# Banded attention of an attention and feed-forward chain: shared-key value products by column halves, the group's result finished over three steps, and copies of P on two engines

## Chip, core and metric

The kernel runs on one core of one Trainium2 chip. The metric is the device time of one execution in microseconds, and the median of 3 runs of the kernel before is 637.89 us (637.67 to 638.56).

## What is computed

```python
def _attn_ref(q, k, v, n_sink, window):          # q, k, v: 2 batches, 8 heads, 768 positions, 64 wide
    scores = np.matmul(q, k.transpose(0, 1, 3, 2)) / np.sqrt(D)
    keep = (pos_k < n_sink) | ((rel >= 0) & (rel < window))      # n_sink 4, window 128
    scores = np.where(keep, scores, -1e9)
    a = np.exp(scores - np.max(scores, axis=-1, keepdims=True))
    return np.matmul(a / (np.sum(a, axis=-1, keepdims=True) + 1e-09), v)

def reference(...):
    x = attention, heads side by side             # 1536 tokens x 512
    h = x @ w_in;  x = softplus(h) @ w_out        # 512 -> 2048 -> 512
    h = x @ w2_in; return (h * clip(h + 3, 0, 6) / 6) @ w2_out
```

## The kernel before

**Attention.** The 1536 tokens are 12 groups `g` of 128 queries (6 blocks `i` in each of 2 batches). A group is worked in two quads of 4 heads, so the loop of `banded_attention` has 24 steps `n` (`g, quad = divmod(n, 2)`) and 3 more in which the pipeline runs empty. For a block other than the first a query sees 208 columns: 128 keys that both halves of the queries share (the upper half of the block before and the lower half of its own), and 80 that belong to one half of the queries (64 of its own and 16 sink keys). Scores are fp32 products (`scores`, L480 and L487) into two PSUM tiles of a pool of three. `exps` takes one head at a time: VectorE adds the mask and takes the row's extreme (L500), ScalarE takes the exponential and its sum (L504). One step later TensorE turns P (`transposes`, L518): four 128x128 pieces into PSUM tile `pt` 0 and four of 80 columns into `pt` 1. VectorE copies the first tile (L526, 128x512), ScalarE the second (L528, 80x512). One step later still come the value products: `apply_x` (L538) for the shared keys, with all 128 queries as the stationary operand, and `apply_y` (L551) for the others, in halves of 64 queries, each half writing its own 64 partitions of the result `o`.

**Finishing a group.** After both quads a group's result is normalised (`normalise`, VectorE, L565), turned (`turn_x`, TensorE, L573, into a third use of the `pt` pool) and split in two parts, `store_hi` (ScalarE, L576) and `store_lo` (VectorE, L580). All four stand in one even step `n`, for group `n // 2 - 2`. `inverse` (L559, L560) prepares the divisors.

**Weights.** In some steps (the table `HALVES`) `w.half()` rebuilds one half block of fp32 weights for the feed-forward part from 64-bit words: three VectorE instructions (L97, L100, L103), one on ScalarE (L107) and one on GpSimd (L108). The raw words come by 512 KB transfers on SyncE's queue (L79, L84), four blocks ahead; the first four are issued in step 1, behind the transfers of queries, keys and values. The 32 half blocks of the first weight pair that attention does not rebuild are rebuilt in the first 16 steps of the feed-forward part (`Ffn.filler`).

**Feed-forward.** Every product of 128x128 by 128x512 is written as three of reduced precision. For each of 16 slices `c`, `products` (L145) makes `h`, `activate` (L167 to L177) the activation, and `stage_b` (L202) adds it to four results two slices later. `h` lives in the same pool of three PSUM tiles as the scores, so `h` of slice `c` waits until VectorE's L175 of slice `c - 3` has read its tile. In steps 24 and 25 of the attention loop `products` of slices 0 and 1 are issued already.

**Order.** A wrapper (`in_order`) keeps each engine's instructions of attention and of the first four feed-forward steps in the order in which the program writes them. Behind that a scheduler orders them.

Of the kernel before, what the change touches and what calls it, by code (L numbers as in the profile page):

```python
# [8 lines left out]
F32 = mybir.dt.float32  # L9
# [4 lines left out]
AF = mybir.ActivationFunctionType  # L14
# [4 lines left out]
P = 128  # L19
NEG = 1.0e9  # L20
MAXSINK = 16
HQ = P // 2
SLOTW = P + MAXSINK
YW = HQ + MAXSINK
PW = P + YW
TB = 2
HALVES = (5, 7, 9, 11, 13, 15, 17, 19, 20, 21, 22, 23)
WARM = 22
FIXED = 4

# [338 lines left out]
def banded_attention(ctx, tc, qT_d, kT_d, v, ident, NSv, Wv, xT, psa, isq, w, ffn, flags):  # L369


    nc = tc.nc
    B, H, D, S = qT_d.shape
    NB = S // P
    NG = B * NB
    NP = H // 2
    NQ = 2 * NG

    one = ctx.enter_context(tc.tile_pool(name="a1", bufs=1))
    two = ctx.enter_context(tc.tile_pool(name="a2", bufs=2))  # L380
# [4 lines left out]
    st = {}  # L385
# [48 lines left out]
    r0, r1 = slice(0, HQ), slice(HQ, P)  # L434
# [23 lines left out]
    def scores(n):  # L458
        g, quad = divmod(n, 2)
        i = g % NB  # L460
        s = st[g]
        if quad == 0:
            s["sum"] = two.tile([P, H], F32, tag="sum", name=f"sum_{g}")
            s["mx"] = two.tile([P, H], F32, tag="mx", name=f"mx_{g}")
        s["P", quad] = two.tile([P, 4, PW], F32, tag="P", name=f"P_{n}")
        s["s", quad] = [psa.tile([P, 2, 256], F32, tag="s", name=f"s_{n}_{t}") for t in range(2)]
        for pp in range(2):
            p = quad * 2 + pp
            if i == 0:
                parts = [None]  # L470
            else:
                parts = [(r0, HQ + MAXSINK, P, 0), (r1, HQ + MAXSINK, PW, 0), (r0, 0, YW, P)]
            for part in parts:
                for t in range(2):
                    rows = slice(t * D, (t + 1) * D)
                    ps = s["s", quad][t]
                    if i == 0:
                        for j in range(2):
                            c0 = j * (HQ + MAXSINK)
                            nc.tensor.matmul(  # L480
                                ps[:, pp, j * HQ : (j + 1) * HQ], s["q"][rows, p, :],
                                keys[rows, p, 0, c0 : c0 + HQ], start=True, stop=True,
                            )
                    else:
                        r, lo, n_, at = part
                        lo += (i - 1) * SLOTW
                        nc.tensor.matmul(  # L487
                            ps[r, pp, at : at + n_], s["q"][rows, p, r],
                            keys[rows, p].rearrange("p i c -> p (i c)")[:, lo : lo + n_], start=True, stop=True,
                        )  # L490

    def exps(n, hh):
        g, quad = divmod(n, 2)
        i = g % NB
        s = st[g]
        w_ = P if i == 0 else PW
        mask = m_zero if i == 0 else m_one if i == 1 else m_gen
        h = quad * 4 + hh
        xs = thr.tile([P, PW], F32, tag="xs", bufs=4, name=f"xs_{n}_{hh}")[:, 0:w_]
        nc.vector.tensor_tensor_reduce(  # L500
            out=xs, in0=s["s", quad][hh % 2][:, hh // 2, 0:w_], in1=mask, scale=-isq, scalar=3.0e38,
            op0=ALU.add, op1=ALU.min, accum_out=s["mx"][:, h : h + 1],
        )
        nc.scalar.activation(  # L504
            s["P", quad][:, hh, 0:w_], xs, AF.Exp, scale=-1.0, bias=s["mx"][:, h : h + 1],
            accum_out=s["sum"][:, h : h + 1],
        )

    def transposes(n):

        g, quad = divmod(n, 2)
        i = g % NB
        s = st[g]
        pt = s["P", quad]
        for m, c0, rows in ((0, 0, P), (1, P, YW)) if i else ((0, 0, P),):
            s["ps", m] = pst.tile([P, 512], F32, tag="pt", name=f"pt_{n}_{m}")
            for hh in range(4):
                nc.tensor.transpose(s["ps", m][0:rows, hh * P : (hh + 1) * P], pt[:, hh, c0 : c0 + rows], ident)  # L518

    def copies(n):  # L520
        g, quad = divmod(n, 2)
        s = st[g]
        for m, rows in ((0, P), (1, YW)) if g % NB else ((0, P),):
            t = two.tile([rows, 512], F32, tag=f"PT{m}", name=f"PT_{n}_{m}")
            if m == 0:
                nc.vector.tensor_copy(t, s["ps", m])  # L526
            else:
                nc.scalar.activation(t, s["ps", m][0:rows], AF.Copy)  # L528
            s["T", quad, m] = t

    def apply_x(n):
        g, quad = divmod(n, 2)
        s = st[g]
        if "o" not in s:
            s["o"] = pso.tile([P, H, D], F32, tag="o", name=f"o_{g}")
        for hh in range(4):
            h = quad * 4 + hh
            nc.tensor.matmul(  # L538
                s["o"][:, h, :], s["T", quad, 0][:, hh * P : (hh + 1) * P], s["vx"][:, h, :],
                start=(hh == 0 or g % NB == 0), stop=(g % NB == 0),  # L540
            )

    def apply_y(n):
        g, quad = divmod(n, 2)
        s = st[g]
        if g % NB == 0:
            return
        for hh in range(4):
            h = quad * 4 + hh
            for j, r in enumerate((r0, r1)):  # L550
                nc.tensor.matmul(  # L551
                    s["o"][r, h, :], s["T", quad, 1][:, hh * P + j * HQ : hh * P + (j + 1) * HQ],
                    s["vy"][:, j, h, :], start=False, stop=(hh == 3),
                )

    def inverse(g):
        s = st[g]
        s["rs"] = two.tile([P, H], F32, tag="rs", name=f"rs_{g}")
        nc.vector.tensor_scalar(out=s["rs"], in0=s["sum"], scalar1=1.0e-9, scalar2=None, op0=ALU.add)  # L559
        nc.vector.reciprocal(s["rs"], s["rs"])  # L560

    def normalise(g):
        s = st[g]
        s["x"] = two.tile([P, H, D], F32, tag="x", name=f"x_{g}")
        nc.vector.tensor_tensor(  # L565
            out=s["x"], in0=s["o"], in1=s["rs"].rearrange("p (h o) -> p h o", o=1).to_broadcast([P, H, D]), op=ALU.mult
        )

    def turn_x(g):
        s = st[g]  # L570
        s["xtr"] = pst.tile([P, NP, P], F32, tag="pt", name=f"xtr_{g}")
        for p in range(NP):
            nc.tensor.transpose(s["xtr"][:, p, :], s["x"][:, 2 * p : 2 * p + 2, :].rearrange("p h d -> p (h d)"), ident)  # L573

    def store_hi(g):
        nc.scalar.activation(xT[:, 0, :, g * P : (g + 1) * P], st[g]["xtr"], AF.Copy)  # L576

    def store_lo(g):
        cols = slice(g * P, (g + 1) * P)
        nc.vector.tensor_tensor(  # L580
            out=xT[:, 1, :, cols], in0=st[g]["xtr"], in1=xT[:, 0, :, cols].bitcast(F32), op=ALU.subtract
        )

    def keep_busy(n):

        for _ in range(n):
            nc.tensor.matmul(spare, z[:, 0:P], z, start=True, stop=True)  # L587
# [23 lines left out]
    for n in range(NQ + 3):  # L611
        g, quad = divmod(n, 2)
        new, old, older = n < NQ, 0 <= n - 1 < NQ, 0 <= n - 2 < NQ
        done = n // 2 - 2 if n % 2 == 0 and n >= 4 else None
        if new:
            scores(n)
        elif n - NQ < 2:
            ffn.products("w1", 0, n - NQ)
        if done is not None:
            normalise(done)  # L620
        if n == 0:
            keep_busy(6)
        if new:
            exps(n, 0)
            exps(n, 1)
        if old:
            transposes(n - 1)
            copies(n - 1)
        if new:
            exps(n, 2)  # L630
            exps(n, 3)
        if done is not None:
            turn_x(done)
        if older:
            apply_x(n - 2)
        if done is not None:
            store_hi(done)
        if older:
            apply_y(n - 2)
        if n % 2 == 0 and n >= 2 and n // 2 - 1 < NG:  # L640
            inverse(n // 2 - 1)
        if done is not None:
            store_lo(done)
        if quad == 1 and new:
            if g % NB == 0:
                spread_sinks()
            if g + 2 < NG:
                fetch_v(g + 2)
            if g + 3 < NG:
                fetch(g + 3)  # L650
            if g == 0:
                w.fetch()
        if n == 0:
            masks(1)
        if n == 2:
            flags()
        if n == NQ:
            ffn.activate("w1", "softplus", 0, 0, lambda: None)
        if n in HALVES:
            w.half()  # L660


def dense_attention(ctx, tc, qT_d, kT_d, v, ident, NSv, Wv, xT, isq):
# [112 lines left out]
```

## Time and profile before

| | |
|---|---|
| median of 3 runs | 637.89 us |
| profiled execution | 638.31 us, of which the span from first to last instruction is 636.5 us |
| busy: TensorE, its weight loads | 619.1 us (97%), 513.0 us (81%) |
| busy: VectorE, ScalarE, GpSimd | 329.5 us (52%), 324.9 us (51%), 206.5 us (32%) |
| first feed-forward product starts | 99.42 us |

The profile is of one execution. A busy share over the whole span mixes attention (to about 110 us), in which four engines share the work, with the feed-forward part, in which TensorE is busy nearly all the time. Durations of TensorE's instructions overlap, since they are pipelined: what one costs is the distance from start to start, which the chain of waits shows. The same holds for VectorE and ScalarE to a smaller degree.

### The profile page before, as it was taken

Reading aid. Unit: us, or ns where it says so; the run is one execution under the profiler, and the core shown is the slowest. Engines: PE = TensorE matmul, PEld = TensorE weight load, DVE = VectorE, ACT = ScalarE, POOL = GpSimd, SP = SyncE. Lnnn points to the kernel's source line nnn. Section 1 sums busy time; section 2 is a strip of 40 time slices with the busy share of each in tenths; the row PEclk is TensorE's granted clock in tenths of the full one; section 3 lists DMA queues with packets and bytes.
Section 4 is the critical chain, followed back from the end, with each engine's and each line's share of the span. In section 5 each row is a group of like instructions: output and inputs, shape, how many; then the busy total and the mean of one; then the engine's idle time right before and its main releaser. Section 6 shows DMA issues by size and latency. Waiting matters only on the chain.

```text
span 636.5 us, 9690 instructions
## 1 busy us (share of the span) xinstructions
PE 619.1 (97%) x3612; PEld 513.0 (81%) x3612; DVE 329.5 (52%) x693; ACT 324.9 (51%) x691; POOL 206.5 (32%) x170
## 2 busy tenths in 40 slices
PE   8999889999999999999999999999999999999996
PEld 4888777878888888888888888888888888888884
DVE  5888897899624222235799996222332222322221
ACT  3776766788867655558687853222222222222221
POOL 0011122699854444445889853000000000000000
PEclk9999999999999999999999999999999999999998
DMA  7996776800000000015656530000010000100001
GB/s 192 266 255 175 212 240 231 299 2 1 1 0 2 0 1 0 1 38 161 197 181 198 186 100 1 1 0 1 13 54 2 0 1 0 67 0 1 1 0 71
DMA packets 46599, 50.12 MB, mean 79 GB/s; under 512 B 15248, under 2 KB 37776, under 8 KB 46544
## 3 DMA queue, kind: packets, MB, share of 16 engines
q1 hardware_dynamic: 45312, 49.16, 25.1%
q8 instruction: 30, 0.49, 0.4%
q10 hardware_dynamic: 1232, 0.26, 0.2%
q14 instruction: 25, 0.20, 0.1%
HBM read 46.27 MB, written 3.15 MB: 78 GB/s over the span
## 4 chain that ended last, share of the span: by engine, by line
PE 90%; DVE 5%; issue 2%; ACT 2%; DMA 1%; SPq 0%; DVEq 0%; ACTq 0%
PE y_w L202 40%; PE h_w L145 39%; PE o L538 3%; PE s L487 2%; PE pt L518 2%; PE o L551 2%; DVE x L565 1%; PE spare L587 1%; PE xtr L573 1%; DVE xs L500 1%; DMA raw_w<-in_moe_w_in_dram 1%; PE s L480 1%; DVE t_w L100 0%; DVE PT L526 0%; DVE t_w L103 0%
## 5 line engine op out<-in xcount | busy, mean ns | idle before, releaser
L145 PE MATMUL h_w<-xT,w_w 128*128 128x512 f32 x1152 | 280.8, 389 | 0.8 <-DVE e_w L175 0.8
L145 PEld LDWEIGHTS h_w<-xT,w_w 128*128 128x128 f32 x1152 | 216.0, 188 | 46.1 <-DVE e_w L175 1.3
L202 PE MATMUL y_w<-g_w,w_w 128*128 128x512 f32 x576 | 141.6, 389 | 0.0
L202 PE MATMUL y_w<-w_w,g_w 128*128 128x512 f32 x576 | 138.9, 389 | 0.0
L202 PEld LDWEIGHTS y_w<-w_w,g_w 128*128 128x128 f32 x576 | 108.0, 188 | 23.1 <-ACT g_w L182 0.4
L202 PEld LDWEIGHTS y_w<-g_w,w_w 128*128 128x128 f32 x576 | 108.2, 188 | 22.4
L108 POOL TENSOR_TENSOR w_w<-t_w,w_w 128x512 fp32r<-128x512 f32 x64 | 82.9, 1296 | 103.6 <-ACT w_w L107 103.1
L181 DVE SCALAR_TENSOR_TENSOR h_w<-e_w,h_w 128x512 f32<-128x512 f32 x48 | 33.4, 695 | 89.0 <-ACT e_w L179 89.0
L179 ACT ACTIVATE e_w<-h_w 128x512 f32<-128x512 f32 x48 | 28.7, 597 | 96.4 <-PE h_w L145 94.6
L183 DVE SCALAR_TENSOR_TENSOR g_w<-h_w,g_w 128x512 fp32r<-128x512 f32 x48 | 33.2, 691 | 83.1 <-ACT g_w L182 83.1
L171 POOL TENSOR_TENSOR u_w<-u_w,e_w 128x512 f32<-128x512 f32 x48 | 62.2, 1295 | 39.6 <-ACT u_w L170 39.5
L182 ACT ACTIVATE g_w<-h_w 128x512 fp32r<-128x512 f32 x48 | 28.7, 598 | 90.3 <-PE y_w L202 90.0
L177 POOL TENSOR_TENSOR g_w<-e_w,g_w 128x512 fp32r<-128x512 f32 x48 | 62.1, 1296 | 36.9 <-ACT g_w L176 36.7
L174 DVE SCALAR_TENSOR_TENSOR h_w<-h_w,r_w 128x512 f32<-128x512 f32 x48 | 33.4, 696 | 64.9 <-ACT r_w L172 64.9
L504 ACT ACTIVATE P<-xs,mx 128x208 f32<-128x208 f32 (+1 forms) x96 | 42.8, 447 | 21.9 <-DVE mx L500 21.8
L107 ACT ACTIVATE w_w<-t_w 128x512 fp32r<-128x512 f32 x64 | 40.0, 625 | 22.4 <-DVE t_w L103 22.3
L167 ACT ACTIVATE e_w<-h_w 128x512 f32<-128x512 f32 x48 | 28.4, 591 | 35.9 <-PE h_w L145 28.9
L175 DVE TENSOR_TENSOR e_w<-h_w,u_w 128x512 f32<-128x512 f32 x48 | 32.9, 686 | 24.0 <-POOL u_w L171 24.0
L176 ACT ACTIVATE g_w<-e_w 128x512 fp32r<-128x512 f32 x48 | 30.1, 626 | 28.0 <-DVE e_w L175 19.6
L97 DVE TENSOR_SCALAR m_w<-raw_w 128x512 int32<-128x512 int32 x52 | 36.0, 693 | 8.3 <-DMA raw_w<-in_moe_w_in_dram 3.8
L103 DVE SCALAR_TENSOR_TENSOR t_w<-raw_w,m_w 128x512 int32<-128x512 int32 x52 | 35.5, 683 | 2.7
L100 DVE SCALAR_TENSOR_TENSOR m_w<-raw_w,m_w 128x512 int32<-128x512 int32 x52 | 35.9, 691 | 1.1
(73 smaller groups left out, 471.1 us busy)
## 6 DMA issues: line engine op xcount, KB each, us to landing
raw_w<-in_moe_w_in_dram SPq DMA_DIRECT2D x32, 512.0 KB, 4.7
raw_w<-in_moe_w_out_dram SPq DMA_DIRECT2D x32, 512.0 KB, 4.7
vx<-in_v_dram SPq DMA_DIRECT2D x12, 256.0 KB, 3.9
out_dram<-o SPq DMA_DIRECT2D x12, 256.0 KB, 2.8
q<-in_q_dram SPq DMA_DIRECT2D x11, 256.0 KB, 3.7
keys<-in_k_dram SPq DMA_DIRECT2D x22, 128.0 KB, 4.0
vy<-in_v_dram SPq DMA_DIRECT2D x20, 128.0 KB, 3.7
vy<-in_v_dram SPq DMA_DIRECT2D x20, 32.0 KB, 3.5
```

The costliest lines, as they stand in the source:

```text
L97: nc.vector.tensor_scalar(out=m, in0=hi, scalar1=3, scalar2=0x3FFFFFF8, op0=ALU.logical_shift_left, op1=ALU.bitwise_and)
L100: nc.vector.scalar_tensor_tensor(out=m, in0=hi, scalar=-0x40000000, in1=m, op0=ALU.bitwise_and, op1=ALU.bitwise_or)
L103: nc.vector.scalar_tensor_tensor(out=t, in0=lo, scalar=29, in1=m, op0=ALU.logical_shift_right, op1=ALU.bitwise_or)
L107: nc.scalar.activation(wt[:, 0, :], t.bitcast(F32), AF.Copy)
L108: nc.gpsimd.tensor_tensor(out=wt[:, 1, :], in0=t.bitcast(F32), in1=wt[:, 0, :].bitcast(F32), op=ALU.subtract)
L145: nc.tensor.matmul(h, wt[:, ws, kk * P : (kk + 1) * P], xT[:, xs, kk, t0 : t0 + 512], start=(n == 0), stop=(n == 11),)
L171: nc.gpsimd.tensor_tensor(out=u, in0=u, in1=e, op=ALU.subtract)
L174: nc.vector.scalar_tensor_tensor(out=h, in0=h, scalar=0.0, in1=r, op0=ALU.max, op1=ALU.add)
L177: nc.gpsimd.tensor_tensor(out=glo, in0=e, in1=ghi.bitcast(F32), op=ALU.subtract)
L181: nc.vector.scalar_tensor_tensor(out=h, in0=e, scalar=6.0, in1=h, op0=ALU.min, op1=ALU.mult)
L202: ins = nc.tensor.matmul(y, lhsT, rhs, start=(c == 0 and n == 0), stop=(c == 15 and n == 2))
L504: nc.scalar.activation(s["P", quad][:, hh, 0:w_], xs, AF.Exp, scale=-1.0, bias=s["mx"][:, h : h + 1], accum_out=s["sum"][:, h : h + 1],)
```

## The change

`apply_x` and `apply_y` become one `apply`, in which the products with the shared keys are made in two halves of 64 queries too: 8 products of 128x64 in place of 4 of 128x128. The three stages of finishing a group are spread: `normalise` at the end of even step `n` for group `n/2 - 2`, `turn_x` and `store_hi` in the next step, `store_lo` in the step after that. Within a step all four `exps` stand together ahead of the copies. The copy of `pt` 0 is split by columns: VectorE copies 256, ScalarE the other 256. `products` of a third slice moves into the attention loop, ahead of the last group's turning. `HALVES` has 11 entries where it had 12: the odd steps from 3 to 23.

```diff
-HALVES = (5, 7, 9, 11, 13, 15, 17, 19, 20, 21, 22, 23)
+HALVES = (3, 5, 7, 9, 11, 13, 15, 17, 19, 21, 23)
...
+    def copies(n, engine):
...
+        if engine is nc.vector:
+            s["T", quad, 0] = two.tile([P, 512], F32, tag="PT0", name=f"PT_{n}_0")
+            nc.vector.tensor_copy(s["T", quad, 0][:, 0 : 2 * P], s["ps", 0][:, 0 : 2 * P])
+            return
+        nc.scalar.activation(s["T", quad, 0][:, 2 * P :], s["ps", 0][:, 2 * P :], AF.Copy)
+        if g % NB:
+            s["T", quad, 1] = two.tile([YW, 512], F32, tag="PT1", name=f"PT_{n}_1")
+            nc.scalar.activation(s["T", quad, 1], s["ps", 1][0:YW], AF.Copy)
+
+    def apply(n):
...
+        for m, rows in ((0, P), (1, YW)) if i else ((0, P),):
+            for hh in range(4):
+                h = quad * 4 + hh
+                for j, r in enumerate((r0, r1)):
+                    nc.tensor.matmul(
+                        s["o"][r, h, :], s["T", quad, m][:, hh * P + j * HQ : hh * P + (j + 1) * HQ],
+                        s["vy"][:, j, h, :] if m else s["vx"][:, h, :],
+                        start=(m == 0 and (hh == 0 or i == 0)), stop=(i == 0 or (m == 1 and hh == 3)),
+                    )
...
     for n in range(NQ + 3):
-        done = n // 2 - 2 if n % 2 == 0 and n >= 4 else None
+        late = n >= NQ
+        ready = n // 2 - 2 if n % 2 == 0 and n >= 4 else None
+        turned = (n - 5) // 2 if n % 2 and n >= 5 else None
         if new:
             scores(n)
-        elif n - NQ < 2:
+        else:
             ffn.products("w1", 0, n - NQ)
-        if done is not None:
-            normalise(done)
...
         if old:
             transposes(n - 1)
-            copies(n - 1)
+        if turned is not None:
+            turn_x(turned)
+        if older:
+            apply(n - 2)
+        if late and ready is not None:
+            normalise(ready)
         if new:
-            exps(n, 2)
-            exps(n, 3)
-        if done is not None:
-            turn_x(done)
-        if older:
-            apply_x(n - 2)
-        if done is not None:
-            store_hi(done)
-        if older:
-            apply_y(n - 2)
+            for hh in range(4):
+                exps(n, hh)
+        if old:
+            copies(n - 1, nc.vector)
+            copies(n - 1, nc.scalar)
+        if ready is not None and not late:
+            normalise(ready)
+        if turned is not None:
+            store_hi(turned)
+        if ready is not None and ready >= 1:
+            store_lo(ready - 1)
...
+    turn_x(NG - 1)
+    store_hi(NG - 1)
+    store_lo(NG - 1)
```

How it moves instructions, at the three places that the prediction speaks of:

VectorE in step 16, an even one in the middle of attention, from the copy of P to the end of the step; `x` is the normalised result, `xtr` the turned one, and the number behind the name is the group. Before:

```order
L526 COPY PT_15_0_1209<-pt_15_0_1199 128x512
L500 ISA xs_16_2_1213,mx_8_1175<-s_16_0_1177,m_gen_113 128x208
L500 ISA mx_8_1175 128x1
L500 ISA xs_16_3_1216,mx_8_1175<-s_16_1_1178,m_gen_113 128x208
L500 ISA mx_8_1175 128x1
L559 TENSOR_SCALAR rs_7_1238<-sum_7_1056 128x8
L560 RECIPROCAL rs_7_1238<-rs_7_1238 128x8
L580 TENSOR_TENSOR xT_77<-xtr_6_1219,xT_77 128x4x128
```

The same place with the change:

```order
L500 ISA xs_16_3_1306,mx_8_1254<-s_16_1_1257,m_gen_113 128x208
L500 ISA mx_8_1254 128x1
L525 COPY PT_15_0_1309<-pt_15_0_1270 128x256
L557 TENSOR_TENSOR x_6_1314<-o_6_1147,rs_6_1174 128x512
L572 TENSOR_TENSOR xT_77<-xtr_5_1202,xT_77 128x4x128
L551 TENSOR_SCALAR rs_7_1317<-sum_7_1125 128x8
L552 RECIPROCAL rs_7_1317<-rs_7_1317 128x8
```

The copy has half the columns and stands behind all four heads; the last subtraction reads group 5, turned a step earlier, where it read group 6, turned in the same step; and normalising group 6 moved here from the head of the step.

VectorE at the end of attention, where `x_11` is the last group's normalised result and the first L97 behind it starts the half blocks of the feed-forward part. Before:

```order
L174 SCALAR_TENSOR_TENSOR h_w1_0_0_1730<-h_w1_0_0_1730,r_w1_0_0_1784 128x512
L175 TENSOR_TENSOR e_w1_0_0_1783<-h_w1_0_0_1730,u_w1_0_0_1785 128x512
L565 TENSOR_TENSOR x_11_1821<-o_11_1764,rs_11_1778 128x512
L580 TENSOR_TENSOR xT_77<-xtr_11_1823,xT_77 128x4x128
L97 TENSOR_SCALAR m_w1_5_1_1964<-raw_w1_5_1_1527 128x512
```

With the change:

```order
L174 SCALAR_TENSOR_TENSOR h_w1_0_0_1831<-h_w1_0_0_1831,r_w1_0_0_1884 128x512
L175 TENSOR_TENSOR e_w1_0_0_1883<-h_w1_0_0_1831,u_w1_0_0_1885 128x512
L557 TENSOR_TENSOR x_11_1944<-o_11_1854,rs_11_1879 128x512
L572 TENSOR_TENSOR xT_77<-xtr_10_1909,xT_77 128x4x128
L572 TENSOR_TENSOR xT_77<-xtr_11_1947,xT_77 128x4x128
L97 TENSOR_SCALAR m_w1_6_0_2075<-raw_w1_6_0_1402 128x512
```

The subtractions of the last two groups stand one behind the other, and the first half block behind them is the one before in the row of half blocks (6_0 in place of 5_1).

SyncE's queue behind the first raw weights, where `near` is a flag that the core reads. Before:

```order
L84 DMA raw_w1_0_1_260<-in_moe_w_out_dram 128x1024
L79 DMA raw_w1_2_0_262<-in_moe_w_in_dram 128x4x256
L348 TENSOR_LOAD near_73
L348 ISA x2
L407 DMA vx_3_359<-in_v_dram 128x512
```

With the change:

```order
L84 DMA raw_w1_0_1_261<-in_moe_w_out_dram 128x1024
L79 DMA raw_w1_2_0_263<-in_moe_w_in_dram 128x4x256
L79 DMA raw_w1_8_0_2082<-in_moe_w_in_dram 128x4x256
L348 TENSOR_LOAD near_73
L348 ISA x2
L407 DMA vx_3_370<-in_v_dram 128x512
```

The transfer of raw block 8_0 came to stand fifth among the first ones, ahead of the values of group 3; before, it was issued near the end of attention.

## Rows read from the trace of the kernel before

**Rows 1.** The windows view by stage: busy us by engine, clock, DMA share, GB/s.

```profile
26.00:99.40 73.40, 66.13 (x992) 58.83 (x988) 62.29 (x222) 50.77 (x174) 13.21 (x11) 1.00 0.75 213
...
113.40:132.00 18.60, 17.76 (x79) 14.38 (x77) 17.65 (x29) 14.60 (x27) 14.06 (x12) 1.00 0.69 248
132.00:636.50 504.50, 498.63 (x2196) 412.06 (x2196) 223.59 (x337) 236.61 (x420) 172.46 (x135) 1.00 0.13 40
```

**Rows 2.** The chain of waits through one pair of steps: start us, us, what.

```profile
67.06 0.70 DVE x L565
...
67.80 0.66 PE xtr L573 x4
68.46 0.84 PE o L538 x8
69.30 0.62 PE o L551 x16
69.91 0.86 PE s L487 x20
70.77 1.03 PE pt L518 x8
...
75.14 0.70 DVE x L565
```

**Rows 3.** The chain of waits earlier, a turning that waited for nothing.

```profile
20.85 0.44 PE xtr L573 x4
```

**Rows 4.** Waits up to 190 us: engine, line, releaser: us, times, longest.

```profile
DVE xT L580 <- ACT xT L576: 12.6, 11, 1.4
...
PE xtr L573 <- DVE x L565: 6.7, 11, 0.8
```

**Rows 5.** The timeline of VectorE in that pair: start us, us, engine, line.

```profile
70.97 0.69 DVE L580 TENSOR_TENSOR xT<-xtr,xT 128x512 fp32r<-128x512 f32 x1 [1.14 <-ACT xT L576]
...
71.58 0.36 DVE L500 CUSTOM_DVE_ANT_0 xs<-s,m_gen 128x208 f32<-128x208 f32 x1
...
71.87 0.37 DVE L500 CUSTOM_DVE_ANT_0 xs<-s,m_gen 128x208 f32<-128x208 f32 x1
...
72.17 0.69 DVE L526 COPY PT<-pt 128x512 f32<-128x512 f32 x1
...
72.77 0.36 DVE L500 CUSTOM_DVE_ANT_0 xs<-s,m_gen 128x208 f32<-128x208 f32 x1
```

**Rows 6.** Groups by line, what brackets the half copies: busy us, mean ns.

```profile
L526 DVE COPY PT<-pt 128x512 f32<-128x512 f32 x24 | 16.4, 685 | 0.0
...
L528 ACT ACTIVATE PT<-pt 80x512 f32<-80x512 f32 x20 | 11.5, 574 | 0.0
...
L452 DVE COPY m_one<-m_gen 128x208 f32<-128x208 f32 x1 | 0.3, 268 | 0.0
```

**Rows 7.** The first raw weights' transfer, its last number the us to landing.

```profile
raw_w<-in_moe_w_in_dram SPq DMA_DIRECT2D x1, 512.0 KB, 4.8
```

**Rows 8.** The timeline of SyncE's queue, the issue of that transfer.

```profile
16.71 0.56 SPq L79 DMA_DIRECT2D raw_w<-in_moe_w_in_dram  x1
```

**Rows 9.** The timeline of TensorE, scores of steps 5 and 6.

```profile
22.67 0.93 PE L487 MATMUL s<-keys,q 64*64 64x128 f32 x24
...
26.02 0.93 PE L487 MATMUL s<-keys,q 64*64 64x128 f32 x24
```

**Rows 10.** The timeline of TensorE around the end of attention.

```profile
91.26 0.93 PE L487 MATMUL s<-keys,q 64*64 64x128 f32 x22 [1.47 <-DVE mx L500]
...
99.42 3.02 PE L145 MATMUL h_w<-xT,w_w 128*128 128x512 f32 x12
```

**Rows 11.** The timeline of VectorE around the end of attention.

```profile
112.77 0.69 DVE L580 TENSOR_TENSOR xT<-xtr,xT 128x512 fp32r<-128x512 f32 x1 [1.38 <-ACT xT L576]
113.38 0.68 DVE L97 TENSOR_SCALAR m_w<-raw_w 128x512 int32<-128x512 int32 x1
```

**Rows 12.** The timeline of TensorE in the feed-forward part.

```profile
132.01 3.03 PE L145 MATMUL h_w<-xT,w_w 128*128 128x512 f32 x12 [0.85 <-DVE e_w L175]
```

More of the change, by code (lines that the diff above doesn't have):

```diff
@@ L518, in transposes @@
                 nc.tensor.transpose(s["ps", m][0:rows, hh * P : (hh + 1) * P], pt[:, hh, c0 : c0 + rows], ident)
-    def copies(n):
+    def copies(n, engine):
         g, quad = divmod(n, 2)
         s = st[g]
[L523 to L531, printed above, removed]
+        if engine is nc.vector:
[7 more added lines that the diff above has]
+    def apply(n):
         g, quad = divmod(n, 2)
+        i = g % NB
         s = st[g]
@@ L535, in apply_x @@
             s["o"] = pso.tile([P, H, D], F32, tag="o", name=f"o_{g}")
[L536 to L554, printed above, removed]
+        for m, rows in ((0, P), (1, YW)) if i else ((0, P),):
[7 more added lines that the diff above has]
+                    )
     def inverse(g):
@@ L613, in banded_attention @@
         new, old, older = n < NQ, 0 <= n - 1 < NQ, 0 <= n - 2 < NQ
-        done = n // 2 - 2 if n % 2 == 0 and n >= 4 else None
+        late = n >= NQ
+        ready = n // 2 - 2 if n % 2 == 0 and n >= 4 else None
+        turned = (n - 5) // 2 if n % 2 and n >= 5 else None
         if new:
             scores(n)
-        elif n - NQ < 2:
+        else:
             ffn.products("w1", 0, n - NQ)
-        if done is not None:
-            normalise(done)
         if n == 0:
             keep_busy(6)
-        if new:
-            exps(n, 0)
-            exps(n, 1)
         if old:
             transposes(n - 1)
-            copies(n - 1)
-        if new:
-            exps(n, 2)
-            exps(n, 3)
-        if done is not None:
-            turn_x(done)
-        if older:
-            apply_x(n - 2)
-        if done is not None:
-            store_hi(done)
-        if older:
-            apply_y(n - 2)
+        if turned is not None:
[4 more added lines that the diff above has]
+            normalise(ready)
+        if new:
+            for hh in range(4):
[9 more added lines that the diff above has]
+            store_lo(ready - 1)
         if n % 2 == 0 and n >= 2 and n // 2 - 1 < NG:
             inverse(n // 2 - 1)
-        if done is not None:
-            store_lo(done)
         if quad == 1 and new:
```

## The prediction

> **What bounds the kernel now.** I first read the windows by stage, whose columns are the stretch, its length, then TensorE, its weight loads, VectorE, ScalarE and GpSimd [rows 1]. From 132 us on TensorE is busy 498.63 of 504.5 us: that part can only move as a block. From 113.4 to 132 us VectorE is busy 17.65 of 18.6. In attention, from 26 to 99.4 us, nobody is full: TensorE 66.13 of 73.4, VectorE 62.29, ScalarE 50.77. The granted clock is 1.00, the 2.4 GHz level, in all of them, so no stretch pays for a lower one.
>
> Next the chain of waits, to see why nobody is full [rows 2]. A pair of steps is 75.14 − 67.06 = 8.08 us, since VectorE's normalise opens each pair. TensorE works in it for 0.66 on the turning, twice 0.84 on shared-key products, twice 0.62 on the others, twice 0.86 on scores, twice 1.03 on turning P: about 7.3, less 0.22 which the turning spends waiting (it took 0.44 where it waited for nothing [rows 3]). The two waits that lock the pair are in the list of waits [rows 4]: the turning waits for VectorE's normalise (6.7 us in 11 times), and VectorE's last subtraction waits for ScalarE's part (12.6 us in 11 times, 1.14 each in this pair [rows 5]). So VectorE works about 8.08 − 1.14 = 6.94 per pair, and then stands for a result that TensorE can turn only once VectorE has normalised.
>
> **The change, part by part.**
>
> *Three steps for finishing a group.* No work is removed. Normalising moves to the end of the even step, the turning comes a step later, the last subtraction another step later and reads the group before. Both waits lose their cause: 1.14 of VectorE's pair and the 0.22 of TensorE's turning. Behind a subtraction without a wait stand VectorE's divisors and next heads, so TensorE's scores get their tiles sooner too.
>
> *Column halves for the shared keys.* Per step 4 products of 128x128 go (8 records in the row, 0.84 us, 105 ns a record) and 8 of 128x64 come, 16 records. No row shows the form. Bounds: 38 ns a record, as for the products of 80x64 weights (0.62 for 16), gives 0.61 a step; 105 ns gives 1.68. The nearest row is the 80x64 one: same columns of weights, same 64 columns moved, same output partitions, only 80 rows in place of 128. I take 0.61, that is −0.23 a step, with 0.84 as the worse case inside the range. By the Trainium skill ("TensorE: Matmul & The Clock Gate", LDWEIGHTS) a weight load takes as many ns as the columns divided by 1.2, whatever the rows. An estimate from that page is 53 ns for 64 columns, and the halves would then cost 0.85 a step, no gain; its rule says that rows don't count, which the choice of the 80x64 row needs, while its figure is above the 38 ns that this row shows. By the one the sum is as below, by the other some 5 us later.
>
> *Copy of P on two engines.* VectorE's copy of 512 columns has a pitch of 0.60 (72.17 to 72.77 [rows 5]); a copy of 256 is between 0.27 (128x208) and 0.60 [rows 6]. I take 0.33 for VectorE, near the 208-column row, and for ScalarE, whose 512 columns take 0.57, 0.30. The two halves come one behind the other, as ScalarE's waits for VectorE's. That costs nothing while the products that read them come a step later; if that slack goes it costs 0.30 a step.
>
> *The pair after the change.* TensorE: 2 x (0.86 + 1.03 + 0.61 + 0.61) + 0.44 = 6.66. VectorE: 6.94 − 2 x 0.27 = 6.40. ScalarE: 50.77 x 8.08 / 73.4 + 2 x 0.30 = 6.2 [rows 1]. The bound passes to TensorE, at 6.66 instead of 8.08, and VectorE has 0.26 to spare.
>
> *Half block in step 3.* The rebuilding enters at step 3, ahead of the heads of step 4 in VectorE's order. Its raw words are issued at 16.71 [rows 8] and land 4.8 later [rows 7], at 21.5; the three passes take 1.8 (pitch 0.6 each), to 23.3. Then three heads at 0.29 [rows 5] free the tile for the scores of step 5: 24.2 instead of 22.67 [rows 9]. Behind the refilling (0.93 + 1.03 + 0.44 + 1.22 on TensorE and about 0.5 of waiting for ScalarE) the scores of step 6 start at about 28.4, where they started at 26.02: 2.4 us lost once.
>
> *Attention to the first feed-forward product.* From step 6 to the first product are 9 pairs: before 99.42 − 26.02 = 73.4 [rows 9, 10]; 9 x 8.08 is 72.7, so the rest is 0.7 of extra rebuilding in steps 20 to 23, which the change thins out. After: 9 x 6.66 = 59.9, the first product at 28.4 + 59.9 = 88.3, so 11.1 earlier.
>
> *End of attention.* TensorE then does three products of a slice (12 at 498.63 / 2196 = 0.227 each, 2.72 [rows 1]), with the last turnings and value products between: 3 x 2.72 + 1.03 + 2 x 1.22 + 0.44 + 0.66, then ScalarE's 0.57 and VectorE's 0.61, 13.9. The last subtraction ends at 102.2; before it ended at 113.38 [rows 11]: again 11.1 to 11.2 earlier.
>
> *Up to the steady feed-forward part.* From 113.38 VectorE rebuilds, without a pause, until its L175 frees the tile for the fourth slice at 132.01 [rows 1, 11, 12]. The same number of blocks and activations stands there after the change, one block earlier in the row, so the 18.6 us stay. The third slice's product lies ahead, but its place in the sum is taken by the same work. The 12th half block (1.8 of VectorE) moves behind, where VectorE is busy 223.59 of 504.5: nothing.
>
> *Moved transfers.* The 512 KB of block 8_0 now go out among the first ones, ahead of the flag and the values of group 3. At 4.8 a transfer, keys and values behind it come up to 4.8 later; their steps are some us off. I take nothing, with up to 4 at the upper end.
>
> Sum: −11.1, and 1.1 back for waits that a tightly packed pair will still have (an estimate: the pair of [rows 2] holds 8.08 − 7.3 = 0.8 besides TensorE's rows, of which I keep 0.12 for each of 9 pairs). That is −10.0. The profiled execution took 638.31, 0.42 above the median: it would be 628.3, and the median **627.9 us**.
>
> **Rivals.** 0.2%, 1.3 us, is about what a measurement of this kernel can tell from no change.
>
> B, *halves as dear as full products*: 0.84 a step instead of 0.61, 20 steps with 0.23 is 4.6: **632.5**. For it: twice as many instructions. Against it: the 80x64 row.
>
> C, *transfers too late*: attention moves its bytes in 73.4 us at a DMA share of 0.75 [rows 1]; in 62.3 the share is 0.88. The mean still fits (at full share 55 us), but a key or raw block that lands 4 late stops all engines: **632**. The stall at 21 to 24 us, longer than the longest wait behind 26 us (1.47 [rows 10]), may also lower the clock, of which no row shows an instance; at half the clock until step 6, 4 us of work, that costs as much.
>
> D, *the pair is better yet*: the seventh group has no 80-column products, which 9 x 6.66 counts in full (0.61 a step and half of the turning of P, about 1.8), and the 1.1 for waits may not come, nor all of the 2.4: **624**.
>
> E, *slower*: each half costs what a full product does, 105 ns a record, because its 128 rows and not its columns set the time. Then 1.68 a step, a pair of 8.80 on TensorE, 1.07 x 20 = 21 more: **649**. The point from which it decides: 10 us over 320 records, 31 ns above 38, so from about 69 ns a record there is no gain left. For it: 105 ns is the only row with 128 rows. Against it: the scores and the 80x64 products show that short instructions come closer together than that.
>
> F, *the change doesn't do what it says*: ScalarE's half, behind its exponentials, comes so late that the products wait for it, and the lock only changes its name. Then the pair ends at 7.9 or so: **637**, no change.
>
> **Chances.** A, the forecast, 626 to 630: 0.54. B 0.13, C 0.12, D 0.11, E 0.07, F 0.03. The range reaches over A, B, most of D and the near half of C: 622 to 634. Faster by over 0.2% in A to D: 0.90; within it F, 0.03; slower E, 0.07.
>
> **What would show it.** Right: a pair of 6.7 to 6.8 in the chain, nearly all of it TensorE; no wait of the last subtraction for ScalarE; 16 records of shared-key products in 0.6; the first feed-forward product near 88 us and the last subtraction near 102; the part behind it as long as before. Wrong, and at which step: 0.84 or more for those records (B, E); a wait of TensorE for ScalarE's copy (F); a wait for keys or raw words, or a granted clock below 1.00 (C); scores of step 6 before 27 us (D).

## Result and the profile after

The changed kernel takes 628.16 us (median of 4 runs, 627.77 to 629.34) where the kernel before takes 638.22 (637.67 to 639.07): a ratio of 0.9844, 95% interval 0.9826 to 0.9862, or 10.1 us. 627.9 was forecast. The profiled execution took 628.13, its span is 626.3.

The windows view of the kernel after, cut at the places that the prediction named (scores of step 6, the first feed-forward product, the first half block behind attention, the product for which VectorE's L175 frees a tile; columns as in [rows 1]):

```profile
29.30:87.30 58.00, 56.81 (x1134) 50.00 (x1132) 55.11 (x224) 53.74 (x195) 11.95 (x10) 1.00 0.89 255
87.30:101.50 14.20, 14.20 (x126) 11.49 (x122) 6.28 (x13) 7.82 (x16) 3.87 (x3) 1.00 0.84 287
101.50:120.10 18.60, 15.78 (x67) 12.15 (x66) 17.66 (x29) 14.60 (x27) 14.03 (x12) 1.00 0.60 211
120.10:626.30 506.20, 500.25 (x2196) 413.06 (x2196) 225.96 (x340) 237.26 (x421) 173.44 (x136) 0.99 0.13 40
```

In attention TensorE is now busy 56.8 of 58.0 us, VectorE 55.1 and ScalarE 53.7; before it was 66.1 of 73.4 [rows 1]. The stretch from 101.5 to 120.1 is as long as it was, 18.6 us, and VectorE fills it as before, 17.66. The last stretch is 506.2 us where it was 504.5.

The chain of waits of the kernel after, around one step with a turning in it (start us, us, what):

```profile
63.63 0.34 DVE PT L525
...
65.31 1.06 PE pt L518 x8
66.37 0.44 PE xtr L565 x4
66.81 1.08 PE o L542 x32
67.89 0.95 PE s L487 x20
...
70.19 0.34 DVE PT L525
70.53 0.60 DVE x L557
71.13 0.60 DVE xT L572
...
72.37 1.24 ACT P L504 x5
```

From 65.31 it stays on TensorE for one step, then it passes to VectorE and ScalarE. Over the nine pairs (29.3 to 87.3) its 58 us are some 26 on TensorE, 16 on ScalarE and 9 on VectorE, the rest gaps and a transfer; before, of 73 us, it was 46, 3 and 13. VectorE's own pair, from one copy of P to that of two steps later, takes 6.56 (63.63 to 70.19) with hardly a gap; TensorE's takes 6.38 where it waits for nothing (29.28 to 35.66 below). The engines are nearly level. Both value products of a step take 1.08 together, where they took 0.84 + 0.62 [rows 2]; the group's turning takes 0.44, its price without a wait [rows 3].

The list of waits up to 190 us of the kernel after (columns as in [rows 4]):

```profile
DVE t_w L97 <- DMA raw_w<-in_moe_w_in_dram: 3.8, 1, 3.8
PE s L487 <- DVE mx L500: 3.6, 1, 3.6
PE h_w L145 <- DVE e_w L175: 2.8, 2, 2.5
DVE xT L572 <- ACT xT L568: 2.6, 2, 2.2
```

The subtraction waits for ScalarE twice, for the last two groups, and no longer 11 times; the turning's wait for VectorE is not in the list at all. What is new: one wait of VectorE for raw words, 3.8 us, one of TensorE's scores behind it, 3.6 (before, the longest of these was 1.5), and a wait of 2.5 us of a feed-forward product for L175, which was 0.85 [rows 12].

The timeline of TensorE of the kernel after at those places:

```profile
24.27 0.93 PE L487 MATMUL s<-keys,q 64*64 64x128 f32 x22 [3.57 <-DVE mx L500]
25.13 1.98 PE L518 MATMUL pt<-ident,P 128*128 128x128 f32 x8
26.90 1.06 PE L565 MATMUL xtr<-ident,x 128*128 128x128 f32 x4
27.89 1.00 PE L542 MATMUL o<-vx,PT 128*64 128x64 f32 x16
...
29.28 0.94 PE L487 MATMUL s<-keys,q 64*64 64x128 f32 x24
...
33.12 1.09 PE L518 MATMUL pt<-ident,P 128*128 128x128 f32 x8
34.04 0.60 PE L565 MATMUL xtr<-ident,x 128*128 128x128 f32 x4
34.57 0.69 PE L542 MATMUL o<-vx,PT 128*64 128x64 f32 x16
35.09 0.64 PE L542 MATMUL o<-vy,PT 80*64 80x64 f32 x16
35.66 0.93 PE L487 MATMUL s<-keys,q 64*64 64x128 f32 x24
...
87.34 3.02 PE L145 MATMUL h_w<-xT,w_w 128*128 128x512 f32 x12
...
120.11 4.63 PE L145 MATMUL h_w<-xT,w_w 128*128 128x512 f32 x12 [2.45 <-DVE e_w L175]
```

From 25.13 to 28.72 the same work takes up to twice as long as ten us later: turning P 1.98 and 1.09, the group's turning 1.06 and 0.60, the products 1.00 and 0.69. The product at 120.11 takes 4.63 where 3.03 was usual. The windows view at both places tells why (the first number behind the brackets of the five engines is the granted clock):

```profile
22.00:24.00 2.00, 0.00 (x0) 0.00 (x0) 1.97 (x7) 0.73 (x2) 0.01 (x1) 1.00 0.87 323
24.00:26.00 2.00, 1.73 (x26) 1.42 (x26) 1.97 (x11) 2.00 (x10) 1.26 (x1) 0.80 1.09 368
26.00:28.00 2.00, 2.00 (x11) 1.57 (x12) 1.97 (x9) 2.00 (x8) 0.00 (x0) 0.50 1.10 304
...
120.00:122.00 2.00, 1.89 (x6) 1.50 (x7) 1.96 (x5) 1.16 (x2) 2.00 (x3) 0.69 0.02 4
122.00:124.00 2.00, 2.00 (x6) 1.53 (x5) 1.86 (x4) 1.81 (x4) 2.00 (x3) 0.50 0.00 0
```

TensorE stood still from 20.7 to 24.3 and from 117.7 to 120.1, and after each of the two its clock was granted at 0.50, the 1.2 GHz level, for some us. In the kernel before it was 1.00 there.

| us from the start of the span | before | forecast | after |
|---|---|---|---|
| scores of step 6 | 26.02 | 28.4 | 29.28 |
| first feed-forward product | 99.42 | 88.3 | 87.34 |
| first half block behind attention | 113.38 | 102.2 | 101.48 |
| product that waits for L175 | 132.01 | 120.8 | 120.11 |
| end of the span | 636.5 | 626.5 | 626.3 |

The forecast's own column is worked out from its text: 102.2 + 18.6 = 120.8, and 628.3 − 1.8 for the last row, which also holds the 1.1 for waits in the pairs.

### The profile page after: what moved, and what is told of

It reads as the page before. It is cut to its first block, busy times and chain, and to the rows that moved or that the text cites. A ratio compares the mean times of both kernels' runs of the same rounds, so it can differ in the third digit from the quotient of the medians.

```text
span 626.3 us, 10133 instructions
## 1 busy us (share of the span) xinstructions
PE 611.6 (98%) x3804; PEld 503.3 (80%) x3804; DVE 322.6 (51%) x693; ACT 329.1 (53%) x715; POOL 206.2 (33%) x170
## 4 chain that ended last, share of the span: by engine, by line
PE 87%; DMA 4%; ACT 3%; DVE 2%; SPq 2%; issue 1%; ACTq 0%; DVEq 0%
PE h_w L145 41%; PE y_w L202 40%; PE pt L518 2%; PE o L542 2%; ACT P L504 2%; DMA raw_w<-in_moe_w_out_dram 1%; DMA vx<-in_v_dram 1%; PE s L487 1%; DMA q<-in_q_dram 1%; DMA raw_w<-in_moe_w_in_dram 1%; DVE xs L500 1%; PE xtr L565 1%; DMA vy<-in_v_dram 0%; ACT w_w L107 0%; PE s L480 0%
## 5 line engine op out<-in xcount | busy, mean ns | idle before, releaser
L145 PE MATMUL h_w<-xT,w_w 128*128 128x512 f32 x1152 | 283.7, 391 | 2.8 <-DVE e_w L175 2.8
L175 DVE TENSOR_TENSOR e_w<-h_w,u_w 128x512 f32<-128x512 f32 x48 | 33.0, 687 | 31.1 <-POOL u_w L171 30.9
L167 ACT ACTIVATE e_w<-h_w 128x512 f32<-128x512 f32 x48 | 28.4, 592 | 37.1 <-PE h_w L145 31.8
L107 ACT ACTIVATE w_w<-t_w 128x512 fp32r<-128x512 f32 x64 | 39.9, 623 | 13.9 <-DVE t_w L103 13.7
L97 DVE TENSOR_SCALAR m_w<-raw_w 128x512 int32<-128x512 int32 x53 | 36.7, 692 | 8.0 <-DMA raw_w<-in_moe_w_in_dram 3.8
```

The source lines that it names most:

```text
L97: nc.vector.tensor_scalar(out=m, in0=hi, scalar1=3, scalar2=0x3FFFFFF8, op0=ALU.logical_shift_left, op1=ALU.bitwise_and)
L107: nc.scalar.activation(wt[:, 0, :], t.bitcast(F32), AF.Copy)
L145: nc.tensor.matmul(h, wt[:, ws, kk * P : (kk + 1) * P], xT[:, xs, kk, t0 : t0 + 512], start=(n == 0), stop=(n == 11),)
```

## Experiments

All medians and ratios stand against runs of the kernel before on the same chip; 1 us is 0.16% of it.

### Which part of the change brings the time

Four kernels take the parts apart. Order alone (both edits undone in the changed kernel):

```diff
-            nc.vector.tensor_copy(s["T", quad, 0][:, 0 : 2 * P], s["ps", 0][:, 0 : 2 * P])
+            nc.vector.tensor_copy(s["T", quad, 0], s["ps", 0])
             return
-        nc.scalar.activation(s["T", quad, 0][:, 2 * P :], s["ps", 0][:, 2 * P :], AF.Copy)
...
+        for hh in range(4):
+            h = quad * 4 + hh
+            nc.tensor.matmul(
+                s["o"][:, h, :], s["T", quad, 0][:, hh * P : (hh + 1) * P], s["vx"][:, h, :],
+                start=(hh == 0 or i == 0), stop=(i == 0),
+            )
-        for m, rows in ((0, P), (1, YW)) if i else ((0, P),):
+        for m, rows in ((1, YW),) if i else ():
```

> The changed kernel with the shared-key products whole again (4 of 128x128 a step) and the first tile of P copied whole by VectorE: of the change there remain the finishing over three steps, the order within a step and the table of half blocks. Theory (the lock between VectorE, TensorE and ScalarE was the bound, and the order alone breaks it): a pair costs about 7.0 us on TensorE (6.4 now, and 2 x 0.32 for the dearer products) and 6.94 on VectorE, so about 6 us behind the changed kernel and 4 ahead of the one before: 634. Rival (the order gives nothing unless products and copies are cheaper): 637 to 639.

Measured: 635.26, ratio 0.9954 (0.9939 to 0.9970).

The second and third kernel take only the last hunk (whole products) or only the first (whole copy).

> The changed kernel with the shared-key products whole again, all else as changed. Theory (TensorE bounds the pair now): 0.32 us a step dearer over some 18 steps on the path, about 6 us behind the changed kernel: 634, the same as with the order alone, since VectorE's cheaper copy only gives it slack. Rival (VectorE or ScalarE bounds the pair as well): 628 to 630.

Measured: 634.16, ratio 0.9934 (0.9912 to 0.9956).

> The changed kernel with the first tile of P copied whole by VectorE, the column halves of the products kept. Theory (VectorE has no slack left beside TensorE): VectorE's pair is 6.4 + 0.54 = 6.94 where TensorE's is 6.4, so VectorE becomes the bound and about 5 us are lost: 633. Rival (VectorE had slack): 628 to 629.

Measured: 631.07, ratio 0.9876 (0.9857 to 0.9895).

The fourth is the kernel before with the halves alone:

```diff
-            nc.tensor.matmul(
-                s["o"][:, h, :], s["T", quad, 0][:, hh * P : (hh + 1) * P], s["vx"][:, h, :],
-                start=(hh == 0 or g % NB == 0), stop=(g % NB == 0),
-            )
+            for j, r in enumerate((r0, r1)):
+                nc.tensor.matmul(
+                    s["o"][r, h, :], s["T", quad, 0][:, hh * P + j * HQ : hh * P + (j + 1) * HQ], s["vx"][:, h, :],
+                    start=(hh == 0 or g % NB == 0), stop=(g % NB == 0),
+                )
```

> The kernel before with the shared-key products in column halves, its order kept. Theory (the pair is locked by VectorE, whose wait for ScalarE does not depend on the products): no more than 1 to 2 us gained, 636 to 638, and the wait of the last subtraction stays. Rival (the products stand on the path, as the chain of the kernel before shows them): 0.32 x 20 = 6 us gained, 632.

Measured: 638.36, ratio 0.9990 (0.9981 to 1.0000): nothing, or a quarter of a us. Its list of waits up to 190 us still has both locks, as large as in [rows 4]:

```profile
DVE xT L581 <- ACT xT L577: 12.6, 11, 1.4
...
PE xtr L574 <- DVE x L566: 6.5, 10, 0.9
...
PE s L487 <- DVE mx L500: 5.8, 8, 2.2
```

TensorE finished its products sooner and waited for VectorE instead, 5.8 us in 8 times, in scores; a pair still takes 8.09 (73.55 to 81.64 in its timeline), where it took 8.08.

Taken together: halves alone 0.25 us; order alone 3.4; order and copies 4.5; order and halves 7.5; all three 10.1. The halves are worth 0.25 in the old order and 635.26 − 631.07 = 4.2 in the new one. The timelines say the same by pairs. Scores with the order alone, two steps apart:

```profile
72.49 0.93 PE L487 MATMUL s<-keys,q 64*64 64x128 f32 x24
...
79.61 0.93 PE L487 MATMUL s<-keys,q 64*64 64x128 f32 x24
```

and with order and halves:

```profile
77.93 0.93 PE L487 MATMUL s<-keys,q 64*64 64x128 f32 x24
...
84.80 0.93 PE L487 MATMUL s<-keys,q 64*64 64x128 f32 x24
```

They are 7.12 and 6.87 us apart, with all three 6.37 to 6.52 in six of the nine pairs. The first is TensorE's sum with whole products, and splitting the copy there changes nothing (whole_products has 73.49 to 80.61, again 7.12); the second is VectorE's sum with a whole copy, 6.94 in the forecast. So the bound passes from the lock to TensorE, then to VectorE; with all three parts the two are level, and ScalarE, whose work no run changes alone, is on the chain too. The whole copy cost less than its expectation said, 2.9 us and not 5 (2.5 when each kernel is taken against the runs of the kernel before on its chip); part of that is in its profile, where the product behind the wait for L175 took 3.01 and not 4.63.

### The last subtraction back in the step of its turning

```diff
         if turned is not None:
             store_hi(turned)
-        if ready is not None and ready >= 1:
-            store_lo(ready - 1)
+            store_lo(turned)
```

> The changed kernel with the last subtraction of a group back in the step of its turning (directly behind ScalarE's part), all else as changed. Theory (the gain of the order is the wait of the last subtraction for ScalarE): ScalarE's part stands behind four exponentials and two copies, about 2.6 us into the step, where VectorE gets there after 1.5, so VectorE waits 1.1 to 1.6 a pair with the half block behind it; its pair goes from 6.4 to 7.5 to 8, and 9 to 13 us are lost: 637 to 641. Rival (VectorE's order no longer matters once TensorE is the bound): 628 to 630.

Measured: 646.23, ratio 1.0119 (1.0103 to 1.0134): 18 us more than the changed kernel, and 8 more than the one before. Its list of waits:

```profile
DVE xT L572 <- ACT xT L568: 24.6, 12, 2.3
...
PE s L487 <- DVE mx L500: 13.1, 9, 3.9
```

The wait is back, 12 times and 2.05 us each, and ScalarE's part now stands behind four exponentials and two copies; a pair takes 8.77 (41.95 to 50.72 and 84.42 to 93.19 in TensorE's scores). The theory's place was right and its size too small. Where the subtraction stands decides alone over more than the whole gain of the change.

### The half block in step 3

```diff
-HALVES = (3, 5, 7, 9, 11, 13, 15, 17, 19, 21, 23)
+HALVES = (5, 7, 9, 11, 13, 15, 17, 19, 21, 23)
```

> The changed kernel with the table of half blocks beginning at step 5 (10 entries in place of 11). Theory (the half block in step 3 makes VectorE wait 3.8 us for raw words, and everything behind it, and the clock falls after the standstill): both go, scores of step 6 start about 5 us earlier, and the eleventh half block costs nothing in the feed-forward part, where the same amount of rebuilding stands ahead of the seventh slice either way: 623 to 624. Rival (what attention does not rebuild VectorE owes in the stretch behind attention, which it bounds): 1.8 us of it come back, 625. Rival (the raw words are late at step 5 too): 627 to 628.

Measured: 628.95 (627.0 to 632.0), ratio 0.9847 (0.9819 to 0.9874). None of the three expectations named what happened, though the last comes near the time. Scores of step 6 did start at 23.57, 5.7 us earlier than in the changed kernel. Then, in the timeline of TensorE:

```profile
23.57 0.93 PE L487 MATMUL s<-keys,q 64*64 64x128 f32 x24
...
34.66 2.02 PE L487 MATMUL s<-keys,q 64*64 64x128 f32 x24 [4.28 <-DMA keys<-in_k_dram]
...
47.48 0.39 PE L542 MATMUL o<-vx,PT 128*64 128x64 f32 x6 [2.04 <-issue]
```

The scores of step 8 wait 4.28 us for keys, the products at 47.48 stand another 2.04, for what the profile doesn't show, and the clock falls to 0.50 behind both (the scores take 2.02 in place of 0.93). The 5.7 us are given back. The order of SyncE's queue shows two raw blocks from the end of attention, 6_1 and 8_0, hoisted to the first transfers, where the changed kernel has one. In the timeline of that queue they are issued ahead of the late keys:

```profile
19.90 0.52 SPq L84 DMA_DIRECT2D raw_w<-in_moe_w_out_dram  x1
20.46 0.43 SPq L79 DMA_DIRECT2D raw_w<-in_moe_w_in_dram  x1
...
29.74 2.70 SPq L400 DMA_DIRECT2D keys<-in_k_dram  x2
```

The next kernel adds spare products in the later standstill, at 120 us (the section on the clock has the edit):

> Both: half blocks from step 5, and the spare products ahead of the seventh slice. Theory: the two gains add, 5 and 1.6: 621 to 622. Rival (one of them has nothing to gain any more, the wait ahead of the seventh slice being another one): no better than the better of the two alone.

Measured: 626.09, ratio 0.9798 (0.9784 to 0.9813); the keys are late there too, 2.22 us at 33.78. The two gains don't add to 6.6: it is 2 us below the changed kernel. Then only the transfers were put back at the end of attention:

```diff
+        if n == 23:
+            w.ahead = 6
+            w.fetch()
+            w.ahead = 4
```

> Half blocks from step 5 and the spare products, as in half5_keep_late, and the two raw blocks 6_1 and 8_0 issued at the end of attention again (the look-ahead is raised to 6 blocks in step 23 for one call) instead of among the first transfers. Theory (the 1 MB of them delayed the keys of the fifth group): the wait of 2 to 4 us of the scores of step 8 for keys goes or shrinks, 624. Rival (keys wait for something else, their buffer or the queue's own order): 626.

Measured: 622.33, ratio 0.9748 (0.9735 to 0.9762). The longest wait for keys is 0.93, and the 3 to 4 us between these two kernels are what the place of the two transfers costs. And with a look-ahead of two raw blocks until step 14:

```diff
-        w = Weights(nc, body.enter_context(tc.tile_pool(name="wt", bufs=1)), 4)
+        w = Weights(nc, body.enter_context(tc.tile_pool(name="wt", bufs=1)), 2)
...
+        if n == 14:
+            w.ahead = 4
```

> The same, and only two raw blocks looked ahead until step 14 instead of four, which takes another 1 MB from the early transfers. Theory (the transfers of the first 35 us are what holds attention's start): no wait for keys or values is left, steps of 3.25 us from step 6 (23.6) on, the first feed-forward product at about 82: 621 to 622. Rival (raw blocks then come late for VectorE): waits of its L97 for raw words, 624 to 627.

Measured: **620.96**, ratio 0.9732 (0.9718 to 0.9746), faster than both kernels: by 17 us and by 7. TensorE's timeline of it:

```profile
23.46 0.93 PE L492 MATMUL s<-keys,q 64*64 64x128 f32 x24
...
81.40 3.06 PE L145 MATMUL h_w<-xT,w_w 128*128 128x512 f32 x12
...
114.22 3.03 PE L145 MATMUL h_w<-xT,w_w 128*128 128x512 f32 x12 [0.30 <-DVE e_w L175]
```

No wait for keys is left, and the spare products fill most of the later standstill; from 23.46 to 81.40 is 57.9 us, the same 58 as in the changed kernel, only six earlier.

Does the one hoisted block cost the changed kernel anything? The same edit (with 5 for 6) in it, half blocks from step 3:

> The changed kernel, half blocks from step 3 on, with nothing altered but that raw block 8_0 is issued at the end of attention, where the kernel before had it (the look-ahead is raised to 5 blocks in step 23 for one call). Theory (as predicted, the moved transfer costs nothing there, since VectorE's wait for the first raw words ends later than the keys land): 628, the first feed-forward product at 87 to 88.5. Rival (it delays keys and raw words of the changed kernel as it did with half blocks from step 5): 625 to 626, and the wait for raw words is 1 to 2 us shorter.

Measured: 628.12, ratio 0.9837 (0.9823 to 0.9850): nothing, as the prediction's sum had it. VectorE's wait for the first raw words is shorter, 2.4 us in place of 3.8, but the scores of step 6 start at 29.08 all the same, with the clock down to 0.57 between 24 and 28 us.

### The clock

Spare products in the standstill at 21 us:

```diff
...
+        if n == 5:
+            st[2]["ps", 0] = pst.tile([P, 512], F32, tag="pt", name="pt_4_0")
+            for _ in range(13):
+                nc.tensor.matmul(st[2]["ps", 0], z[:, 0:P], z, start=True, stop=True)
```

> The changed kernel with 13 spare products (128x128 by 128x512, zeros) ahead of the scores of step 5, in the standstill of about 3.6 us; the wait for raw words stays. Theory (the fallen clock lengthens the work behind the standstill): the granted clock stays 1.00 there, turning P, the group's turning and the value products behind it take 1.1 + 0.6 + 0.7 in place of 2.0 + 1.1 + 1.0, 1.2 to 1.7 us gained: 626.5 to 627. Rival (that work waits for ScalarE's exponentials, whatever the clock): 628.

Measured: 627.37, ratio 0.9817 (0.9801 to 0.9833). Windows and timeline of TensorE:

```profile
24.00:26.00 2.00, 1.33 (x25) 0.95 (x24) 2.00 (x11) 1.83 (x7) 1.12 (x1) 1.00 1.09 372
26.00:28.00 2.00, 1.91 (x17) 1.27 (x14) 1.97 (x13) 2.00 (x9) 0.15 (x1) 1.00 1.09 310
```

```profile
21.15 2.98 PE L613 MATMUL pt<-z 128*128 128x512 bf16 x13
...
25.16 0.93 PE L487 MATMUL s<-keys,q 64*64 64x128 f32 x22 [0.67 <-DVE mx L500]
...
29.07 0.94 PE L487 MATMUL s<-keys,q 64*64 64x128 f32 x24
...
120.01 3.06 PE L145 MATMUL h_w<-xT,w_w 128*128 128x512 f32 x12 [2.46 <-DVE e_w L175]
```

The clock stays at 1.00, and from the scores of step 5 to those of step 6 it takes 3.91 us (25.16 to 29.07) in place of 5.01 (24.27 to 29.28): between these two executions 1.1 us is what the fallen clock costs there. That the scores of step 6 start at nearly the same time lies in the raw words, which came 0.9 later in this execution. In the times the gain is within the intervals.

Spare products ahead of the seventh slice:

```diff
...
+            if s == 5 and self.zz is not None:
+                for _ in range(10):
+                    self.nc.tensor.matmul(self.y["w1", 0, 0], self.zz[:, 0:P], self.zz, start=False, stop=False)
```

> The changed kernel with 10 spare products of zeros added to an open result ahead of the seventh slice of the feed-forward part, in the wait of 2.45 us for VectorE's L175. Theory (the clock falls after that wait and costs 1.6 us, since from there on TensorE alone sets the end): the granted clock stays 1.00 there, the slice takes 3.0 in place of 4.6: 626.5. Rival (VectorE is behind anyway, and the next slice waits for it instead): 628.

Measured: 627.60, ratio 0.9828 (0.9815 to 0.9842), within the interval of the changed kernel. The slice took 3.04 and the clock stayed at 1.00. But that doesn't prove the remedy: keep_early's last row above is the same product behind the same wait, without spare products there, and takes 3.06. In the profiles the wait of 2.43 to 2.49 us was followed by the lower level three times (the changed kernel, order_only, no_early_8_0: 4.5 to 4.6 us) and not five times (whole_products, whole_copy, lo_same_step, half_step5, keep_early: 3.0 to 3.1). What decides is open; it makes 1.5 us between executions. From that product to the end of the span it is 506.2 us with the fall and 504.3 without (keep_early), before 504.5.

## Why the prediction was right

**The lock and its end: right.** Both waits of [rows 4] are gone, and lo_same_step shows what the place of the subtraction does: with everything else as changed, its wait is back and 18 us with it. The turning's wait for VectorE stays away there but for 0.4 us; normalising and turning were not put back by themselves.

**The new bound: right in part.** With dearer products TensorE bounds the pair (whole_products, 6.0 us lost), with a dearer copy VectorE does (whole_copy, 2.9). But the forecast left VectorE 0.26 to spare and named as its sign a pair that is nearly all TensorE in the chain. That sign failed: some 26 of the 58 us are TensorE's. Its pair became cheaper than forecast and is level with VectorE's, and ScalarE, busy 53.7 of 58, holds 16 us of the chain.

**The price of the halves: mis-sized, to the good.** 0.61 a step was taken for each kind of product. The chain shows 1.08 for both, from the timeline 0.51 or 0.52 for the shared keys (34.57 to 35.09) and 0.57 for the others. So TensorE's own pair is 6.37 in place of 6.66. 128 rows cost no more than 80, and rival E's 105 ns a record is far off: it is 0.51 / 16 = 32 ns, and 0.57 / 16 = 36 with 80 rows. The halves also write another half of the output from one product to the next, which the whole products did not; no run separates that from the columns. The Trainium skill ("TensorE: Matmul & The Clock Gate", LDWEIGHTS) says of a weight load that rows don't count and columns do. The trace agrees on the rows; the 53 ns for 64 columns, an estimate by its formula, taken as the spacing of records doesn't agree: 32 ns measured, and the measurement decides.

**Half block in step 3: right place, the price too small.** The raw words landed at 21.36 (21.5 forecast), the scores went on at 24.27 (24.2). But they reached step 6 at 29.28, not 28.4: the clock, which rival C named for just this standstill, was left out of the sum. It cost 1.1, by keep_early.

**The end of attention and the stretch behind it: right.** 14.1 and 18.6 us; 13.9 and 18.6 were forecast. One name was wrong: the product that the tile of the fourth slice frees is that of the seventh slice, not of the fourth. The argument (the same blocks and activations ahead of it) holds for it. The reading of the kernel before had one slip that the sum doesn't use: the 0.7 put down to extra rebuilding in steps 20 to 23 is a balance over nine uneven pairs, of which the last took 10.06 (89.36 to 99.42 in TensorE's timeline).

**The last stretch: 1.7 us not foreseen.** The text took it as a block that only moves. The wait ahead of it grew from 0.85 to 2.45, since TensorE came to it with less work left over (busy 15.78 of the 18.6 us, where it was 17.76), and in this execution the clock fell behind it. No row of before showed such a wait, and no term asked what TensorE does while VectorE sets the time.

**Why the sum still came out.** Against the forecast of 628.3 for the profiled execution: 0.9 for step 6, −2.9 for the nine pairs with their waits (59.9 and 1.1 forecast, 58.06 measured from 29.28 to 87.34), 0.2 for the end of attention, 1.7 behind it; together −0.1. The −2.9 is a sum itself, of estimates from the timeline's rows: −2.6 for the cheaper pair; about −1.7 for the seventh group, which has no 80-column products and which 9 x 6.66 counted in full; and about 1.3 for waits, which came to 2.4 in place of 1.1. Most of these waits, about 1.8, fall right behind the seventh group, where two pairs take 5.52 and 7.37 (54.93 to 60.45 to 67.82) and the chain runs on VectorE and ScalarE for long. Errors of either sign cancel, and that the total came within 0.3 us is luck; the steps are the evidence.

**Rivals.** B and E fell with 32 ns a record, F with the list of waits (TensorE waits for ScalarE's copy 0.5 us in all), though the chain does pass through that copy. C was half there: its clock came, its late keys did not. half_step5, without the stall and with a second block hoisted, shows them come; that the stall alone kept them away is not shown. D was right on the seventh group and a cheaper pair, and wrong that the waits might not come.

## What to carry to other kernels

When two engines hand a result to and fro inside one step, cheaper instructions buy nothing (0.25 us for the halves in the old order); put the steps of the exchange one turn of the loop apart first, then the same edit is worth 4 to 6 us. An instruction that waits for another engine belongs where that engine's queue has surely passed the result: one line in the wrong place cost 18 us. And look at what a stall was hiding before it is removed: here it was late transfers, and the cure was in their order on the queue: 626.09 to 620.96, 5 of the 7 us by which the fastest kernel beats the changed one.

## What was not expected of the hardware

Products with 64-column halves come every 32 ns a record with 128 rows of weights, where whole ones came every 105 ns in [rows 2]. A standstill of TensorE of 2.43 to 2.49 us was followed by the 1.2 GHz level in three profiled executions and not in five others, with the same instructions around it; in halves_only one of 2.22 us at the end of attention was followed by it too (granted clock 0.60 and 0.54 from 92 to 96 us). A profile of one execution can be 1.5 us off by that alone.
